# One more 2 MB load and store, in rows of 16 KB, ahead of everything else in a decode-attention backward kernel

## The chip, the core and the metric

The kernel runs on one core of a Trainium2 chip. Five engines work side by side: TensorE (PE, with its weight loads as PEld), VectorE (DVE), ScalarE (ACT), GpSimd (POOL) and SyncE (SP), which here issues nearly all transfers. Sixteen DMA engines move the data between HBM and the on-chip memory of 128 partitions. The metric is the device time of one execution in microseconds.

## What is computed

The reference is the forward pass and the gradients of a block that adds two branches to its input: attention of one new token over a cache, and a bilinear gated MLP.

```
def _A_ref(x, k_cache, v_cache, wq, wo):          # B=2, Sq=1, D=576, Hq=32, Hkv=16, Sk=4096, Dh=128
    q = (x @ wq).reshape(B, Sq, Hq, Dh).transpose(0, 2, 1, 3)
    k, v = jnp.repeat(k_cache, rep, axis=1), jnp.repeat(v_cache, rep, axis=1)      # rep = 2
    p = softmax(jnp.einsum("bhqd,bhkd->bhqk", q, k) * Dh ** -0.5)
    o = jnp.einsum("bhqk,bhkd->bhqd", p, v)
    return o.transpose(0, 2, 1, 3).reshape(B, Sq, Hq * Dh) @ wo
def _B_ref(x, w_gate, w_up, w_down):              # F = 4608
    return ((x @ w_gate) * (x @ w_up)) @ w_down
xn = layernorm(x)
out = x + _A_ref(xn, k_cache, v_cache, wq, wo) + _B_ref(xn, w_gate, w_up, w_down)
```

There are nine outputs: `out` (out_0) and the gradients by x (out_1), the key cache (out_2), the value cache (out_3), wq (out_4), wo (out_5), w_gate (out_6), w_up (out_7) and w_down (out_8). All is bfloat16. The two caches are 2 x 16 x 4096 x 128, 33.5 MB each, and so are their gradients; every gradient has the size of its input, so as many bytes are written as read.

## The kernel before, in words

**Steps.** The work on the caches is cut into 16 steps. A step is one group of two key heads (four query heads) of one of the two batch rows. For each step two heads of keys and two of values are loaded, 1 MB per head: partition p holds 32 consecutive positions, which is one row of 8 KB (`load_kv`, line 1078; the transfer is on line 1087). DVE transposes them in blocks (`turn`, through the helper on line 418), PE makes the scores (line 1205), the softmax runs on ACT and DVE, PE contracts the probabilities with the cache (line 1378), and PE makes the gradients of keys and values as outer products (line 1226). Their results stand in PSUM in pieces of 128 x 1024 and are copied to a big buffer by ACT or DVE (the helper `cp`, lines 422 and 424), whichever the planner picks, and stored from there (`put`, line 644). In between stand the groups of weights of attention (wq, wo) and nine slices of the MLP, whose gradients are outer products too.

**Buffers.** Sixteen big buffers of 8 KB per partition (`big`, line 368) are shared by four users: loaded keys and values (`kv`, at most 7 at a time), transposed copies (`X`, at most 15), results to be stored (`st`, at most 4) and gate or up weights (`G`, at most 2). A buffer is taken with ACQ and given back with REL, or, for a transfer, when the transfer has landed.

**Order.** All parts of the kernel are generators, which yield what they need next: an engine for an estimated time, a buffer, an event, a transfer. A planner (`Order`, line 64) runs them at build time against its own estimates and a table of priorities (`PRI`, line 256), takes what can start first, and so writes down the order of instructions on each engine. The order is fixed when the program is built; at run time each engine works through its list, and waits on semaphores. One added request can so move everything that is planned after it.

**Queues.** SP issues all transfers but two small ones of ACT, in one list. It does not pass over an entry: a store that waits for its eviction holds up the loads behind it. Transfers use eight completion semaphores in turn, so a transfer is issued only once the one eight places before it has landed. The list of before starts with the first head of keys, the first weights of wq and wo, the second head of keys and the first head of values, then two MB of gate and up weights and two slices of w_down, the second head of values, and the keys and values of the next step. The first store stands behind 20 transfers.

Of the kernel before, what the change touches and what calls it, by code (L numbers as in the profile page):

```python
# [12 lines left out]
BF16 = mybir.dt.bfloat16  # L13
P = 128
# [210 lines left out]
def ACQ(tag):  # L225
    return ("acq", tag)
# [6 lines left out]
def WAIT(*events):  # L233
    return ("wait", events)


def SET(event):
    return ("set", event)
# [6 lines left out]
def PRIO(prio):  # L245
    return ("prio", prio)


def DMA(engine, cost, nbytes, row=8192):
    return ("dma", engine, cost, 0.01 + RATE * nbytes / 16e3 * (0.03676 + 8.0 / row))  # L250
# [3 lines left out]
NBIG, NGU, NWW, NBD = 16, 1, 6, 3  # L254
# [51 lines left out]
def pr(name, i=0):  # L306
    return PRI[name][i]
# [3 lines left out]
def kernel(  # L311
# [22 lines left out]
    nc = tc.nc  # L334

    Bq, Sq, D = A_x.shape
    _, Hkv, Sk, Dh = A_k_cache.shape
# [8 lines left out]
    NCH = Sk // P  # L346
# [12 lines left out]
    const = ctx.enter_context(tc.tile_pool(name="const", bufs=1))  # L359
    ps = ctx.enter_context(tc.tile_pool(name="ps", bufs=1, space=bass.MemoryType.PSUM))  # L360

    od = Order()

    def tiles(tag, n, shape, dtype=BF16):
        od.ring(tag, n)
        return [const.tile(list(shape), dtype, name=f"{tag}{i}") for i in range(n)]

    kv_t = X_t = st_t = G_t = tiles("big", NBIG, [P, NCH * Dh])
    od.share("big", CAP)
    Xt_t = tiles("Xt", 1, [P, 2 * FS])  # L370
    gu_t = tiles("gu", NGU, [P, 4 * FS])
# [703 lines left out]
    views = [A.rearrange("b h (p c) d -> b h p (c d)", p=P) for A in (A_k_cache, A_v_cache)]  # L1075
    oviews = [A.rearrange("b h (p c) d -> b h p (c d)", p=P) for A in (out_2, out_3)]

    def load_kv():
        n = 0
        for s in range(NS):  # L1080
            g, b = divmod(s, Bq)
            for t in range(2):
                for l in range(G):
                    yield PRIO(pr("load", s) if n else -1e5)
                    i = yield ACQ("kv")
                    yield DMA("SP", 0.36, 1 << 20)
                    nc.sync.dma_start(kv_t[i][:], views[t][b, G * g + l])
                    kvS[s][t][l] = i
                    yield ("lset", kvL[s][t][l])
                    yield SET(issued[n])  # L1090
                    n += 1
# [48 lines left out]
    def load_ws(items):  # L1140
        for n, (gate, item) in enumerate(items):
            yield PRIO(pr("mload" if item[0] == "mlp" else "wload", n))
            yield ("gate", issued, gate)
            yield from load_w(item)

    def turn():
        for s in range(NS):
            for t in range(2):
                yield PRIO(pr(f"turn{t}", s))
                for l in range(G):  # L1150
                    yield WAIT(kvL[s][t][l], *([] if s + t == 0 else [grp[s // Bq]["Ed" if t else "Eq"]]))
                    x = yield ACQ("X")
                    src = kv_t[kvS[s][t][l]]
                    for h in range(2):
                        yield DVE(1.25)
                        t32(pairs(X_t[x][:, 2048 * h:2048 * h + 2048]), pairs(src[:, 2048 * h:2048 * h + 2048]))
                    xS[s][t][l] = x
                    yield SET(xE[s][t][l])

    def build_W(t):  # L1160
        for s in range(NS):
            g, b = divmod(s, Bq)
            yield PRIO(pr(f"W{t}", s))
            yield WAIT(Ezero)
            yield WAIT(grp[g]["Eq" if t == 0 else "Ed"])
            w = yield ACQ(f"W{t}")
            wS[s][t] = w
            for a in range(4):
                yield POOL(0.22)
                nc.gpsimd.tensor_copy(  # L1170
                    view(W_t[t][w][:], 32 * a, 32, 6 + 8 * a, [[G * WW, 4], [WW, G], [1, 2]]),
                    view(rep_t[grp[g]["qs"]][:], 32 * a, 32, t * 8 * GH + b, [[2 * GH, 4], [4, G], [2, 2]]))
            yield SET(wE[s][t])

    def build_BD():
        for s in range(NS):
            g, b = divmod(s, Bq)
            for t in (0, 1) if s == 0 else (1, 0):
                yield PRIO(pr(f"BD{t}", s))
                yield WAIT(Econst)  # L1180
                yield WAIT(*[grp[g][x] for x in (("Eq",) if s == 0 and t == 0 else ("Eq", "Ed"))])
                v = yield ACQ("vr")
                m = yield ACQ("m")
                yield PE(0.053)
                nc.tensor.matmul(m_t[m][:, 0:P],
                                 lhsT=qr_t[grp[g]["qs"]][:, t, b, :],
                                 rhs=ident[:], start=True, stop=True)
                e = yield EV(128)
                cp(e, vr_t[v][:], m_t[m][:, 0:P])
                yield REL("m", m)  # L1190
                i = yield ACQ("BD")
                yield POOL(3.6)
                nc.gpsimd.tensor_tensor(BD_t[i][:], view(vr_t[v][:], 0, P, 0, [[0, 16], [1, Dh]]),  # L1193
                                        view(mask16[:], 0, P, 0, [[1, 16], [0, Dh]]), ALU.mult)
                yield REL("vr", v)
                bS[s][t] = i
                yield SET(bE[s][t])
# [50 lines left out]
    def attend():  # L1248
        for s in range(NS):
            yield PRIO(pr("att", s))  # L1250
            yield WAIT(Econst)
            yield from softmax(s)
# [98 lines left out]
    def dscores():  # L1351
        for s in range(NS):
            yield PRIO(pr("dsc", s))
            yield from dscore(s)
# [50 lines left out]
    def backs():  # L1405
        for g in range(NG):
            yield PRIO(pr("back", g))
            yield WAIT(Emore, Exr)
            yield from group_back(g)

    def fronts():
        for g in range(NG):
            yield PRIO(pr("front", g))
            yield from group_front(g)
# [33 lines left out]
    def final_dx():  # L1448
# [46 lines left out]
    od.spawn(load_ws([it for g in range(NG) for it in (  # L1495
        (AT["wq"][g], ("wq", g)), (AT["wo"][g], ("wo", g)))]), -50.0, 0.2)
    od.spawn(load_ws([(AT["mlp"][i], ("mlp", i)) for i in range((NFS + 1) // 2)]), -50.0, 0.2)
    od.spawn(load_kv(), -1e5, 0.0)
    for gen in (turn(), fronts(), build_W(0), build_W(1), build_BD(), attend(), dscores(), backs()):
        od.spawn(gen, 0.0)  # L1500
# [33 lines left out]
```

## Time and profile before

| | before |
|---|---|
| median of two runs | 471.11 us (470.67 to 471.55) |
| profiled execution | 471.37 us |
| its span | 469.6 us |
| mean granted TensorE clock | 0.71 |
| bytes moved | 185.96 MB, mean 396 GB/s |
| data queue, share of 16 engines | 98.1% |
| busiest engines | PE 79%, DVE 79%, ACT 71%, POOL 31% |
| transfers of SP | 220 |

The span runs from the first to the last instruction of one profiled execution; its own time has some 1.8 us more around it. Busy shares are averages over the whole span. The DMA share is the mean over 16 engines of the time that packets were under way; since a packet's time holds its waiting and packets overlap a little, it can stand slightly above 1. In lists of waits, an entry names the engine and line that waited, the engine and line that ended the wait, the total, the number and the longest.

### The profile page before, as it was taken

Reading aid. Unit: us, or ns where it says so; the run is one execution under the profiler, and the core shown is the slowest. Engines: PE = TensorE matmul, PEld = TensorE weight load, DVE = VectorE, ACT = ScalarE, POOL = GpSimd, SP = SyncE. Lnnn points to the kernel's source line nnn. Section 1 sums busy time; section 2 is a strip of 40 time slices with the busy share of each in tenths; the row PEclk is TensorE's granted clock in tenths of the full one; section 3 lists DMA queues with packets and bytes.
Section 4 is the critical chain, followed back from the end, with each engine's and each line's share of the span. In section 5 each row is a group of like instructions: output and inputs, shape, how many; then the busy total and the mean of one; then the engine's idle time right before and its main releaser. Section 6 shows DMA issues by size and latency. Waiting matters only on the chain.

```text
span 469.6 us, 15459 instructions
## 1 busy us (share of the span) xinstructions
PE 370.8 (79%) x6636; PEld 217.5 (46%) x6636; DVE 369.5 (79%) x705; ACT 334.3 (71%) x507; POOL 146.8 (31%) x176
## 2 busy tenths in 40 slices
PE   0588688869887777986997669789699898998984
PEld 0455444435653352554463444564345434444453
DVE  9689878967867879688689658978867978898772
ACT  2149668867885948671798638877678678789973
POOL 3350242681330320203252264000843705325100
PEclk9978897767757668776675767956656658566977
DMA  8999999999999999999999999999999989999995
GB/s 317 404 413 403 363 390 419 409 416 421 418 416 420 399 421 406 412 415 419 399 418 404 386 418 424 408 413 342 413 416 393 424 270 416 423 413 413 424 368 176
DMA packets 40053, 185.96 MB, mean 396 GB/s; under 512 B 3496, under 2 KB 11184, under 8 KB 23600
## 3 DMA queue, kind: packets, MB, share of 16 engines
q1 hardware_dynamic: 39976, 184.96, 98.1%
q8 instruction: 52, 0.85, 0.7%
q14 instruction: 17, 0.14, 0.1%
q10 hardware_dynamic: 8, 0.00, 0.0%
HBM read 92.48 MB, written 92.48 MB: 394 GB/s over the span
## 4 chain that ended last, share of the span: by engine, by line
PE 42%; ACT 18%; DVE 18%; DMA 12%; issue 5%; POOL 2%; SPq 2%; ACTq 0%; DVEq 0%; POOLq 0%
ACT big L422 15%; DMA out_dram<-big 10%; DVE big L418 8%; PE ps_m L1378 8%; PE ps_o L1226 7%; PE ps_m L1205 7%; PE ps_o L675 4%; PE ps_m L841 3%; DVE big L424 3%; DMA big<-in_A_v_cache_dram 3%; PE ps_m L967 2%; PE ps_m L636 2%; POOL BD L1193 2%; PE ps_o L712 1%; SPq L1129 1%
## 5 line engine op out<-in xcount | busy, mean ns | idle before, releaser
L422 ACT CAST big<-ps_o 128x1024 bf16<-128x1024 f32 (+4 forms) x319 | 279.7, 950 | 40.3 <-PE ps_o L1226 18.2
L418 DVE STREAM_TRANSPOSE big<-big 128x1024 f32<-128x1024 f32 x146 | 176.1, 1223 | 5.9 <-DMA big<-in_A_v_cache_dram 3.6
L1193 POOL TENSOR_TENSOR BD<-vr,mask 128x2048 bf16<-128x2048 bf16 x32 | 115.2, 3603 | 198.8 <-ACT vr L422 122.2
L424 DVE CAST big<-ps_o 128x1024 bf16<-128x1024 f32 (+2 forms) x71 | 78.2, 1102 | 15.8 <-PE ps_o L675 5.2
L1205 PE MATMUL ps_m<-big,W 128*32 128x128 bf16 x2048 | 57.1, 274 | 5.5 <-ACT osb L422 0.7
L1226 PE MATMUL ps_o<-BD,dd 32*128 32x512 bf16 x256 | 48.8, 489 | 12.7 <-ACT big L422 9.2
L1205 PEld LDWEIGHTS <-W 128*32 128x32 bf16 x2048 | 45.4, 121 | 21.9 <-issue 18.6
L1226 PE MATMUL ps_o<-BD,pp 32*128 32x512 bf16 x256 | 42.1, 461 | 10.4 <-ACT big L422 6.7
L1170 POOL COPY W<-rep 32x16 bf16<-32x16 bf16 x128 | 24.5, 192 | 63.5 <-DVE rep L951 53.2
L418 DVE STREAM_TRANSPOSE big<-ww 128x1152 f32<-128x1152 f32 (+1 forms) x25 | 32.9, 1317 | 4.5 <-DMA out_dram<-big 3.3
L1378 PE MATMUL ps_m<-big,pp 128*32 128x512 bf16 x256 | 28.2, 536 | 1.5 <-DVE small L1330 1.2
L1378 PE MATMUL ps_m<-big,dd 128*32 128x512 bf16 x256 | 27.5, 518 | 1.5 <-DVE dd L418 0.6
L1226 PEld LDWEIGHTS <-dd 32*128 32x128 bf16 x256 | 11.8, 97 | 32.4 <-issue 24.7
L1226 PEld LDWEIGHTS <-pp 32*128 32x128 bf16 x256 | 10.4, 95 | 26.9 <-issue 22.6
L422 ACT CAST osb<-ps_m 128x512 bf16<-128x512 f32 x15 | 8.9, 590 | 15.9 <-PE ps_m L1378 12.6
L675 PE MATMUL ps_o<-dyr,R 32*32 32x288 bf16 x256 | 17.3, 402 | 2.0 <-ACT big L422 2.0
L675 PE MATMUL ps_o<-dyr,hb 32*32 32x288 bf16 x288 | 16.5, 346 | 1.1 <-ACT big L422 0.9
L967 PE MATMUL ps_m<-big,Wdy 128*128 128x128 bf16 x144 | 14.9, 285 | 3.1 <-DVE small L1283 2.0
L712 PEld LDWEIGHTS <-xnr 32*128 32x128 bf16 x368 | 12.5, 119 | 9.3 <-issue 8.6
L422 ACT CAST sp<-ps_m 128x256 bf16<-128x256 f32 x22 | 8.4, 380 | 11.2 <-PE ps_m L1213 11.0
L636 PEld LDWEIGHTS <-wm 128*32 128x32 bf16 x704 | 13.4, 115 | 6.3 <-issue 5.1
L841 PE MATMUL ps_m<-big,Wdy 128*128 128x128 bf16 x162 | 15.6, 272 | 0.6 <-DVE small L1291 0.4
(210 smaller groups left out, 481.9 us busy)
## 6 DMA issues: line engine op xcount, KB each, us to landing
out_dram<-big SPq DMA_DIRECT2D x74, 1024.0 KB, 12.1
big<-in_A_k_cache_dram SPq DMA_DIRECT2D x32, 1024.0 KB, 12.4
big<-in_A_v_cache_dram SPq DMA_DIRECT2D x32, 1024.0 KB, 12.5
out_dram<-big SPq DMA_DIRECT2D x17, 576.0 KB, 11.4
ww<-in_B_w_down_dram SPq DMA_DIRECT2D x9, 576.0 KB, 11.1
ww<-in_A_wo_dram SPq DMA_DIRECT2D x8, 576.0 KB, 11.1
ww<-in_A_wq_dram SPq DMA_DIRECT2D x8, 512.0 KB, 11.6
big<-in_B_w_gate_dram SPq DMA_DIRECT2D x4, 1024.0 KB, 13.1
```

Source lines behind the costliest of these rows:

```text
L418: nc.vector.transpose(out, in_)
L422: nc.scalar.copy(out, in_)
L424: nc.vector.tensor_copy(out=out, in_=in_)
L636: nc.tensor.matmul(dp[32 * q:32 * q + 32, :], lhsT=view(Wm[:], 0, P, 8 * pos(q, s), [[1, 32]]), rhs=view(X, 0, P, xoff(q, s), [[FS, blocks ...
L675: nc.tensor.matmul(o[32 * q:32 * q + 32, aa, 0:HD2], lhsT=view(t, 32 * q, 32, 2 * A + aa, [[4, 32]]), rhs=dyr[32 * q:32 * q + 32, k * HD2: ...
L841: nc.tensor.matmul(dh, lhsT=Wdy[:, e, 2 * k:2 * k + P], rhs=view(X[:], 0, P, 64 * k + e, [[D, FC], [2, 32]]), start=(k == 0 and e == 0), s ...
L967: nc.tensor.matmul(dp, lhsT=Wdy[:, e, 2 * k:2 * k + P], rhs=view(X[:], 0, P, 64 * k + e, [[D, GH], [2, 32]]), start=(k == 0 and e == 0), s ...
L1170: nc.gpsimd.tensor_copy(view(W_t[t][w][:], 32 * a, 32, 6 + 8 * a, [[G * WW, 4], [WW, G], [1, 2]]), view(rep_t[grp[g]["qs"]][:], 32 * a, 32 ...
L1193: nc.gpsimd.tensor_tensor(BD_t[i][:], view(vr_t[v][:], 0, P, 0, [[0, 16], [1, Dh]]), view(mask16[:], 0, P, 0, [[1, 16], [0, Dh]]), ALU.mult)
L1205: nc.tensor.matmul(sc[32 * cq:32 * cq + 32, :], lhsT=view(W[:], 0, P, (be * G + l) * WW + 6 - 4 * c2 - 2 * l, [[1, 32]]), rhs=view(X[:], 0 ...
L1226: nc.tensor.matmul(o[:, k, :], lhsT=pr2[32 * c4:32 * c4 + 32, :], rhs=BD[32 * c4:32 * c4 + 32, 8 * l + 4 * h2:8 * l + 4 * h2 + 4, :], star ...
L1378: nc.tensor.matmul(ct[32 * j:32 * j + 32, :], lhsT=view(rT, 0, P, 4 * c + 2 * l, [[1, 32]]), rhs=kv_t[kvS[s][t][l]][:, Dh * c:Dh * (c + 4) ...
```

## The change

A new generator `long_rows` is planned ahead of `load_kv`. It takes two neighbouring buffers, loads the first two heads of keys of batch row 0 into them with one transfer of 2 MB, waits until it has landed, and stores the same bytes with one transfer to the place of the last two heads of key gradients of batch row 1. These are written again later, by the stores of the last step, so what the kernel returns does not change. Each of the 128 rows of the two transfers is 16 KB long: partitions 0 to 63 take the first head and 64 to 127 the second, 64 positions each.

So that a row of 16 KB fits, the sixteen big buffers are now the halves of eight tiles of twice the size. Their number, their size and the caps of their users are the same. `load_kv` still loads the same heads of keys again for its own use.

```
-    kv_t = X_t = st_t = G_t = tiles("big", NBIG, [P, NCH * Dh])
+    pair_t = [const.tile([P, 2 * NCH * Dh], BF16, name=f"big{i}") for i in range(NBIG // 2)]
+    kv_t = X_t = st_t = G_t = [t[:, NCH * Dh * h:NCH * Dh * (h + 1)] for t in pair_t for h in range(2)]
+    od.ring("big", NBIG)
...
+    def long_rows():
+        yield PRIO(-2e5)
+        i = yield ACQ("kv")
+        j = yield ACQ("kv")
+        assert j == i + 1 and i % 2 == 0
+        two = pair_t[i // 2]
+        land = Event()
+        yield DMA("SP", 0.36, 2 << 20, 16384)
+        nc.sync.dma_start(two[:], A_k_cache[0, 0:2].rearrange("h (p c) d -> (h p) (c d)", p=P // 2))
+        yield ("lset", land)
+        yield WAIT(land)
+        yield DMA("SP", 0.36, 2 << 20, 16384)
+        nc.sync.dma_start(out_2[1, Hkv - 2:Hkv].rearrange("h (p c) d -> (h p) (c d)", p=P // 2), two[:])
+        yield ("lrel", "kv", i)
+        yield ("lrel", "kv", j)
...
+    od.spawn(long_rows(), -2e5, 0.0)
     od.spawn(load_kv(), -1e5, 0.0)
```

In the built order of the changed kernel the long load is SP's first transfer and the long store its ninth; between them stand the first two heads of keys, wq, wo, the first head of values and the first gate weights.

## The prediction

> **What bounds the kernel now.** I read the page from the outside in: first how full the DMA engines are, then where in the span they are not, and only then the engines and the chain. These are lines of the page of the kernel before: span, engine and slice rows, DMA queues, chain, two groups of evictions, and DMA issues with their time to landing.
>
> ```profile
> span 469.6 us, 15459 instructions
> PE 370.8 (79%) x6636; PEld 217.5 (46%) x6636; DVE 369.5 (79%) x705; ACT 334.3 (71%) x507; POOL 146.8 (31%) x176
> ...
> DMA  8999999999999999999999999999999989999995
> GB/s 317 404 413 403 363 390 419 409 416 421 418 416 420 399 421 406 412 415 419 399 418 404 386 418 424 408 413 342 413 416 393 424 270 416 423 413 413 424 368 176
> DMA packets 40053, 185.96 MB, mean 396 GB/s; under 512 B 3496, under 2 KB 11184, under 8 KB 23600
> ...
> q1 hardware_dynamic: 39976, 184.96, 98.1%
> q8 instruction: 52, 0.85, 0.7%
> ...
> HBM read 92.48 MB, written 92.48 MB: 394 GB/s over the span
> ...
> PE 42%; ACT 18%; DVE 18%; DMA 12%; issue 5%; POOL 2%; SPq 2%; ACTq 0%; DVEq 0%; POOLq 0%
> ...
> L422 ACT CAST big<-ps_o 128x1024 bf16<-128x1024 f32 (+4 forms) x319 | 279.7, 950 | 40.3 <-PE ps_o L1226 18.2
> ...
> L424 DVE CAST big<-ps_o 128x1024 bf16<-128x1024 f32 (+2 forms) x71 | 78.2, 1102 | 15.8 <-PE ps_o L675 5.2
> ...
> out_dram<-big SPq DMA_DIRECT2D x74, 1024.0 KB, 12.1
> ```
>
> The queue that carries the data was taken for 98.1% of the span, and no engine for more than 79%. The slice row says the same thing over time: a 9 everywhere but in the first slice, one in the middle and the last. The chain that ended last looks like compute (PE 42%, ACT 18%, DVE 18%), but I do not read it as the bound. Each load waits for a buffer that a reader frees, and each store for an eviction, so a chain followed back from the end runs through engines even while the DMA engines always have work.
>
> The windows (columns: stretch, length, busy time of PE, PEld, DVE, ACT, POOL, granted clock, DMA share, GB/s) show where the queue falls short.
>
> ```profile
> 0.00:1.90 1.90, 0.00 (x0) 0.00 (x0) 1.10 (x13) 0.32 (x1) 1.30 (x7) 1.00 0.17 31
> ...
> 0.00:35.26 35.26, 17.50 (x334) 12.35 (x334) 27.60 (x96) 11.29 (x25) 14.88 (x27) 0.90 0.96 378
> ...
> 5.00:455.00 450.00, 363.52 (x6450) 212.30 (x6453) 360.38 (x667) 326.45 (x495) 142.52 (x168) 0.71 1.01 405
> ...
> 200.00:300.00 100.00, 80.30 (x1442) 48.91 (x1442) 78.83 (x137) 69.55 (x111) 32.09 (x41) 0.69 1.01 410
> 300.00:400.00 100.00, 84.05 (x1372) 45.54 (x1369) 78.95 (x140) 74.98 (x110) 36.47 (x43) 0.64 0.98 387
> 400.00:455.00 55.00, 49.35 (x787) 25.97 (x783) 46.00 (x81) 47.23 (x68) 13.61 (x4) 0.69 1.02 418
> 455.00:469.60 14.60, 7.29 (x190) 5.13 (x190) 4.92 (x19) 6.40 (x10) 0.00 (x0) 0.73 0.52 182
> ...
> 375.00:380.00 5.00, 4.75 (x60) 2.19 (x58) 4.41 (x8) 3.50 (x5) 0.02 (x1) 0.50 0.59 204
> ```
>
> From 5 to 455 us the share is 1.01: packets lie back to back for 450 of 469.6 us, and in the middle I see one clear hole (375 to 380 us, share 0.59, so 0.41 x 5 = 2.1 us lost). Outside that stretch stand a start-up of about 2 us and a tail of 14.6 us at share 0.52. So bytes set this time: what is added to the queue is paid in full, unless it fills a hole.
>
> The profiled execution took 471.37 us by its own time, 1.8 us more than its span; the median of the runs is 471.11. They differ by 0.06%, so a sum on the profiled one stands for both. A measurement tells 2% from no change here: 9.4 us, or 480.5 us.
>
> **The change, part by part.** *Bytes.* Nothing is removed. Two DMAs come in: a load of 2 MB (2,097,152 bytes, 128 rows of 16 KB) and a store of the same size. The same keys are loaded a second time by the old loop, and the stored rows are overwritten by the last key gradients, so neither replaces other traffic. Together they are 4.19 MB, 2.3% of 185.96 MB.
>
> The price per byte of a 16 KB row of this queue stands in no row of the trace, so I bound it. From below, the best stretch: 400 to 455 us, mostly transfers of 1 MB in 8 KB rows, ran at 418 GB/s, which gives 4.19 / 0.418 = 10.0 us; slices reach 424 GB/s, 9.9 us. From above, the only packets of 16 KB in the trace: the instruction queue moved 52 of 0.85 MB, so 16 KB each, in 0.7% of 16 engines' span, or 0.007 x 16 x 469.6 / 52 = 1.01 us a packet; 256 of them on 16 engines are 16.2 us. The mean of the full stretch, 405 GB/s, gives 10.4. I take 10.0, from the data queue's own large rows: the instruction fetches are isolated packets that share each engine with this queue, so their time holds waiting.
>
> The Trainium skill, in "DMA: Bandwidth & Descriptors" under Specifications, gives about 358 GB/s of HBM per core and says that for HBM traffic this side binds; by it the term would be 11.7 us as an estimate and the sum 483.9 us. The trace disagrees, with 405 GB/s held over 450 us.
>
> *The two issues.* SP issues a transfer in about 0.34 us (the rows below); the median one lands 12.1 us after its issue, so the queue is several transfers deep and this costs nothing. If the queue were dry, it would cost 0.7 us.
>
> *The load stands first.* All other transfers start 2 MB later: 2.1 / 0.418 = 5.0 us. Nothing on the chip waits for these rows except their own store, but the first keys wait behind them. SP's own rows, and the first transpose of keys on DVE (start us, length, what):
>
> ```profile
> 8.31 1.23 DVE L418 STREAM_TRANSPOSE big<-big 128x1024 f32<-128x1024 f32 x1
> ...
> 35.26 0.34 SPq L644 DMA_DIRECT2D out_dram<-big  x1
> ...
> 39.07 0.34 SPq L644 DMA_DIRECT2D out_dram<-big  x1
> ```
>
> Compute so starts about 5 us later, which is part of the 10.0 us and not added to it: DMA is busy meanwhile. The danger is the first store that needs compute. SP issues in order, so a store that waits for an eviction holds back all loads behind it, and those feed DVE and PE. Before, 15.3 MB stand ahead of that store, which went out at 35.26 us, when 35.26 x 0.378 = 13.3 MB had moved: 2.0 MB in hand. In the built order of the changed kernel 16.3 MB stand ahead of it, and it is the value gradient that went out at 39.07 us before. The queue lasts until 35.26 + (16.3 - 13.3) / 0.405 = 42.7 us; the data come at 39.07 + 5.0 = 44.1 us at the latest, and earlier since the evictions of the MLP's store now come behind. The hole is 0 to 1.4 us; I take 0.8, about the middle.
>
> *The long store.* It stands ninth on SP, after three MB of keys, values and gate weights. Its load came first, so its wait is over when SP gets there; behind it are weight loads and the second half of the values. Until it lands, two of the seven buffers for keys and values and two of the sixteen big ones are missing. This moves no bytes, only their order, and loads fill the queue meanwhile. If the cover were gone, it would be one more wait of SP of the length below.
>
> *The order after that.* Instructions are laid out by a planner at build time, so all else may move. Counting bytes ahead of each transfer in both built orders: most of the 64 loads and 64 stores stand 4.2 MB further back, which is a plain shift; loads 45 to 50 stand 5.8 to 6.9 MB back, and loads 23 to 27 about where they were. Behind the last load of values 15.8 MB are left, before it was 16.8. About 12 evictions of the big buffers pass from ACT to DVE: 12 x 1.10 = 13 us more DVE work in 480 us, which is 80% in place of 79%. I cost this part at nothing, since DVE is not the bound; the price when it opens holes is the rival below. The tail (14.6 us at 0.52) I leave as it is.
>
> *Pair tiles.* A big buffer becomes half of a pair. In the built program no wait ties two halves of one pair to each other that are used separately, so they cost nothing.
>
> *Sum:* 471.4 + 10.0 (bytes) + 0.8 (first hole) = 482.2 us, 2.4% above.
>
> **The rivals.** *The bytes are partly absorbed.* The first keys come 5 us late and the whole queue is 10 us longer, so after the long store compute runs some 5 us ahead of the queue compared with before. SP's waits (us in total, times, longest) would shrink:
>
> ```profile
> SPq L644 <- ACT big L422: 112.3, 58, 6.9
> SPq L644 <- DVE big L424: 90.6, 36, 7.9
> SPq L1087 <- PE ps_m L1378: 16.5, 7, 7.8
> ```
>
> The wait of 7.8 us is the one that made the hole at 375 us. If that lead closed the holes, the stretch from 300 to 400 us would run at 410 GB/s like the one ahead of it, not at 387: 100 x (1 - 387/410) = 5.6 us back. The time would be 471.4 + 10.0 - 5.6 = 475.8 us, not slower by what can be told. It decides once more than 1.7 us come back. Against it: buffers, not engines, give the lead, and they are as many as before, so a lead is used up as soon as the buffers are full; and part of the low rate is small rows, not holes. By the same mechanism, with all of the shortfall against 418 GB/s returned (450 x (1 - 405/418) = 14.0 us), the time would be 467.4; 11,184 packets under 2 KB speak against that.
>
> *The new order opens holes.* A wait of SP longer than the queue is deep leaves the engines dry. The queue is 12.1 us deep at the median, the longest wait 7.9 us, and one of 7.8 us made the hole of 2.1 us. With loads 45 to 50 2 MB later and other stores ahead of loads, four such holes more are 8.4 us: 490.6 us. For it: 203 us of waits for evictions lie just under the surface, and each could surface. Against it: the shift by bytes is even.
>
> *Rows of 16 KB are slow.* At the price of the instruction packets: 471.4 + 16.2 + 0.8 = 488.4 us. Against it: those packets wait beside a full queue, and 8 KB at 418 GB/s are 8,192 x 16 / 418,000 = 0.31 us a packet, a third of 1.01 us for half the bytes.
>
> *It does less than it says.* If the two transfers cost only the delay of the first keys, the time would be 476.4 us; it needs idle DMA engines, of which the first slices show none after 1.9 us.
>
> **How the numbers follow.** Forecast 482.2 us: 0.60, its own range 480 to 485, of which about a tenth lies under 480.5. Absorbed: 0.15. New holes: 0.18. Slow rows: 0.05. Less than it says: 0.02. Slower by over 2% is 0.60 x 0.9 + 0.18 + 0.05 = 0.77; faster by over 2% (below 461.7) needs more back than any hole holds, 0.01; within 2% the rest, 0.22. For 8 in 10 the range reaches from 477.5, most of the absorbed case, to 489.5, most of the holes and the slow rows.
>
> **What would show it.** The queue's row: 189.1 MB in q1 and a share near 98%, with GB/s over 5 to 465 us near 405. The first transpose of keys near 13 us instead of 8.3. The long transfers: 256 packets of 16 KB, or 512 of 8 KB, and 5 us each in their stretch. Around 42 us a window with a share below 1. If windows in the middle show shares of 0.6 to 0.9 more often than before, the new order is at work; if 300 to 400 us rises above 400 GB/s, bytes are absorbed. I am wrong if the share stays at 98% and the time rises by clearly more or less than 10 us: then the rate of the rows, not the holes, has changed.

## The result and the profile after

The changed kernel took 493.31 us (median of two runs, 492.31 to 494.31), the kernel before 471.11 us. The ratio is 1.0471, with a 95% interval of 1.0371 to 1.0572: slower by 22.2 us, about twice the 11 us forecast and 3.8 us above the range. The profiled execution took 494.31 us, its span 492.5 us.

The page of the changed kernel: span, engines, slices, queue, and the two groups of evictions.

```profile
span 492.5 us, 15462 instructions
PE 376.3 (76%) x6636; PEld 214.3 (44%) x6636; DVE 384.5 (78%) x725; ACT 323.2 (66%) x487; POOL 147.3 (30%) x176
...
DMA  8997989999998999999989999999999979999995
GB/s 313 409 411 291 395 307 365 391 376 402 422 418 333 366 415 418 424 422 415 419 293 415 416 412 387 420 424 416 364 411 418 425 288 353 418 416 412 421 417 206
DMA packets 40341, 190.15 MB, mean 386 GB/s; under 512 B 3528, under 2 KB 11216, under 8 KB 23632
...
q1 hardware_dynamic: 40264, 189.16, 96.7%
...
L424 ACT CAST big<-ps_o 128x1024 bf16<-128x1024 f32 (+2 forms) x305 | 269.1, 957 | 63.5 <-PE ps_o L1244 39.0
...
L426 DVE CAST big<-ps_o 128x1024 bf16<-128x1024 f32 (+3 forms) x85 | 92.7, 1091 | 23.6 <-PE ps_o L677 7.4
```

The bytes came as announced: 189.16 MB in the data queue, and 40,264 - 39,976 = 288 packets more, of which 256 are the rows of 16 KB. But the queue is less full. Its share times the span gives 476.2 us of packet time, and 16.3 us without; before, 98.1% of 469.6 us were 460.7, and 8.9 without. So of the 22.9 us by which the span grew, 15.5 are packet time and 7.4 are time without packets. Two transfers of 2 MB, priced at 10.0 us of packet time, explain neither the rest of the 15.5 nor the 7.4. (Such sums carry some 2 us: another execution of the same lists, in the run with the nudged estimate below, has 98.1% of 471.4 us, or 462.4.) The slice row has several more digits below 9, spread over the run, and not only at the start.

The windows of the changed kernel (columns as before) show the worst places, and its list of SP's waits what SP stood at.

```profile
40.00:45.00 5.00, 4.11 (x37) 2.29 (x31) 4.21 (x7) 3.52 (x6) 2.73 (x1) 1.00 0.53 220
45.00:50.00 5.00, 5.00 (x138) 3.73 (x137) 2.97 (x6) 3.90 (x6) 0.88 (x1) 1.00 0.91 298
...
155.00:160.00 5.00, 3.57 (x65) 1.71 (x65) 4.91 (x7) 5.00 (x8) 2.19 (x1) 0.86 0.65 215
250.00:255.00 5.00, 2.66 (x22) 0.66 (x22) 5.00 (x6) 4.34 (x5) 0.00 (x0) 0.50 0.69 191
400.00:405.00 5.00, 4.17 (x104) 2.93 (x97) 4.82 (x10) 3.13 (x4) 2.61 (x1) 0.91 0.38 124
405.00:410.00 5.00, 4.02 (x47) 1.34 (x46) 3.90 (x11) 2.76 (x7) 0.77 (x4) 1.00 1.00 365
5.00:455.00 450.00, 347.07 (x6110) 196.51 (x6110) 357.62 (x655) 296.34 (x448) 139.96 (x168) 0.72 0.99 391
```

```profile
SPq L646 <- DVE big L426: 117.1, 42, 12.4
SPq L646 <- ACT big L424: 95.5, 61, 7.8
SPq L1105 <- PE ps_m L1396: 32.1, 9, 10.4
SPq L1105 <- DMA out_dram<-big: 31.9, 11, 12.4
```

From 5 to 455 us the rate is 391 GB/s, where it was 405. Before, SP's longest wait was 7.9 us. Now there are three of 10 to 12.4 us, and each stands beside a hole: the first, 12.4 us at a store that waits for DVE, ends in the hole at 40 us, and one of 10.4 us ends at the hole at 250 us. The hole at 155 us has no such wait. There SP sent four stores in the 15.2 us from 137.8 us on and then stood 4.2 us more, so several shorter waits in a row did the same. The long wait at 400 us is of another kind: SP's own rows around it (start us, length, what) show that nothing was issued for 12 us.

```profile
385.63 4.83 SPq L646 DMA_DIRECT2D out_dram<-big  x4
402.88 0.34 SPq L1105 DMA_DIRECT2D big<-in_A_v_cache_dram  x1
```

Here a load of values takes the buffer of a store that had just been issued, and so waits until that store has landed. Since SP issues nothing meanwhile, the queue drains almost to the end: share 0.38 from 400 to 405 us.

### The profile page after: what moved, and what is told of

The parts are those of the page before. It is cut to its first block, busy times and chain, and to the rows that moved or that the text cites. A ratio compares the mean times of both kernels' runs of the same rounds, so it can differ in the third digit from the quotient of the medians.

```text
span 492.5 us, 15462 instructions
## 1 busy us (share of the span) xinstructions
PE 376.3 (76%) x6636; PEld 214.3 (44%) x6636; DVE 384.5 (78%) x725; ACT 323.2 (66%) x487; POOL 147.3 (30%) x176
## 3 DMA queue, kind: packets, MB, share of 16 engines
q1 hardware_dynamic: 40264, 189.16, 96.7%
## 4 chain that ended last, share of the span: by engine, by line
PE 42%; ACT 18%; DVE 17%; DMA 15%; issue 7%; SPq 1%; DVEq 0%; ACTq 0%
ACT big L424 15%; DVE big L420 9%; PE ps_o L1244 8%; PE ps_m L1223 8%; PE ps_m L1396 7%; DMA big<-in_A_v_cache_dram 7%; PE ps_o L677 4%; DVE big L426 4%; DMA big<-in_A_k_cache_dram 3%; DMA ww<-in_A_wq_dram 3%; DMA out_dram<-big 3%; PE ps_m L969 2%; PE ps_m L638 2%; PE ps_m L843 1%; PE ps_o L714 1%
## 5 line engine op out<-in xcount | busy, mean ns | idle before, releaser
L424 ACT CAST big<-ps_o 128x1024 bf16<-128x1024 f32 (+2 forms) x305 | 269.1, 957 | 63.5 <-PE ps_o L1244 39.0
L426 DVE CAST big<-ps_o 128x1024 bf16<-128x1024 f32 (+3 forms) x85 | 92.7, 1091 | 23.6 <-PE ps_o L677 7.4
L1244 PE MATMUL ps_o<-BD,dd 32*128 32x512 bf16 x256 | 46.4, 464 | 11.8 <-ACT big L424 9.9
L1244 PE MATMUL ps_o<-BD,pp 32*128 32x512 bf16 x256 | 45.9, 502 | 10.6 <-ACT big L424 8.0
L1396 PE MATMUL ps_m<-big,pp 128*32 128x512 bf16 x256 | 29.2, 545 | 5.6 <-DMA big<-in_A_v_cache_dram 4.0
L985 POOL COPY qr<-qd 128x256 bf16<-128x256 bf16 x8 | 3.2, 397 | 54.1 <-DVE qd L426 53.5
L424 ACT CAST sp<-ps_m 128x256 bf16<-128x256 f32 x25 | 9.5, 381 | 13.2 <-PE ps_m L1231 11.0
L714 PEld LDWEIGHTS <-xnr 32*128 32x128 bf16 x368 | 12.7, 115 | 11.6 <-issue 10.9
L843 PEld LDWEIGHTS <-Wdy 128*128 128x128 bf16 x162 | 13.6, 121 | 5.9 <-issue 5.0
## 6 DMA issues: line engine op xcount, KB each, us to landing
out_dram<-big SPq DMA_DIRECT2D x74, 1024.0 KB, 12.7
big<-in_B_w_gate_dram SPq DMA_DIRECT2D x4, 1024.0 KB, 12.4
```

The source lines that it names most:

```text
L424: nc.scalar.copy(out, in_)
L426: nc.vector.tensor_copy(out=out, in_=in_)
L714: nc.tensor.matmul(o[:, aa, j * P:(j + 1) * P], lhsT=xnr[32 * a:32 * a + 32, dc * P:(dc + 1) * P], rhs=rhs(a), start=True, stop=True)
L843: nc.tensor.matmul(dh, lhsT=Wdy[:, e, 2 * k:2 * k + P], rhs=view(X[:], 0, P, 64 * k + e, [[D, FC], [2, 32]]), start=(k == 0 and e == 0), s ...
L1244: nc.tensor.matmul(o[:, k, :], lhsT=pr2[32 * c4:32 * c4 + 32, :], rhs=BD[32 * c4:32 * c4 + 32, 8 * l + 4 * h2:8 * l + 4 * h2 + 4, :], star ...
L1396: nc.tensor.matmul(ct[32 * j:32 * j + 32, :], lhsT=view(rT, 0, P, 4 * c + 2 * l, [[1, 32]]), rhs=kv_t[kvS[s][t][l]][:, Dh * c:Dh * (c + 4) ...
```

## The experiments

Three causes could give 22 us where 10 were priced. *New order*: the bytes cost their packets, the rest comes from the order that the planner laid out anew. *Rows*: the packets of 16 KB disturb the queue. *Late keys*: compute starts late and stays late. Medians and ratios are against runs of the kernel before on the same chip.

| run | median us | before us | ratio, 95% interval |
|---|---|---|---|
| old order, rows of 16 KB | 481.11 | 471.54 | 1.0218 (1.0183 to 1.0253) |
| old order, rows of 8 KB | 482.52 | 471.54 | 1.0235 (1.0210 to 1.0260) |
| new order, no bytes | 484.27 | 471.54 | 1.0268 (1.0216 to 1.0320) |
| latency estimate nudged | 471.72 | 471.54 | 1.0006 (0.9988 to 1.0025) |
| new order, one store later | 491.46 | 471.54 | 1.0416 (1.0390 to 1.0441) |
| no rows, rate estimate 0.3% up | 492.93 | 471.54 | 1.0452 (1.0413 to 1.0492) |
| no rows, drift estimate up | 482.17 | 471.54 | 1.0232 (1.0198 to 1.0265) |
| no rows, planned for late keys | 490.92 | 471.54 | 1.0433 (1.0392 to 1.0475) |
| old order, long load alone | 476.82 | 471.70 | 1.0109 (1.0075 to 1.0143) |
| old order, 13 evictions moved | 475.09 | 471.70 | 1.0068 (1.0037 to 1.0098) |
| new order, split as before | 496.05 | 471.70 | 1.0504 (1.0456 to 1.0551) |

### The bytes without the new order

The planner is not told of the long rows. Its order stays that of before on all engines, and the two transfers are put into SP's list at the places that they have in the changed kernel, through a pair of buffers that is still unused then.

```
+    def spd(dst, src):                     # stands in for every nc.sync.dma_start
+        spn[0] += 1
+        if spn[0] == 1:
+            nc.sync.dma_start(pair_t[7][:], A_k_cache[0, 0:2].rearrange("h (p c) d -> (h p) (c d)", p=P // 2))
+        if spn[0] == 8:
+            nc.sync.dma_start(out_2[1, Hkv - 2:Hkv].rearrange("h (p c) d -> (h p) (c d)", p=P // 2), pair_t[7][:])
+        nc.sync.dma_start(dst, src)
```

> The order of the kernel before on every engine, untouched; only the long load is put in as SP's first transfer and the long store as its ninth, in rows of 16 KB, through two buffers that nothing else uses before 29 us. Theory 'new order' (the bytes cost their packets, 10.7 us, and the other 12 us come from the order that the planner laid out anew): 480 to 484 us. Rival 'rows' (the long packets disturb the queue by more than their own time): 488 to 495 us. Rival 'late keys' (keys that come 5 us late make compute late for the whole run, whatever the order): 487 to 495 us.

The second run moves the same bytes with two loads and two stores of 1 MB, in rows of 8 KB.

> As the run with the old order and rows of 16 KB, but the same 2 MB are loaded and stored as two transfers of 1 MB each way, in rows of 8 KB. Theory 'new order': as with rows of 16 KB, 480 to 484 us. Rival 'rows': 480 to 483 us, 5 us or more below the run with rows of 16 KB. Rival 'late keys': 487 to 495 us, as with rows of 16 KB.

Measured: 481.11 and 482.52 us. Both rivals fall. Rows of 16 KB cost no more than rows of 8 KB (the intervals overlap), and keys that come late do not make the run late. The page of the run with rows of 16 KB, and its windows:

```profile
span 478.3 us, 15465 instructions
...
q1 hardware_dynamic: 40264, 189.16, 98.5%
```

```profile
40.00:45.00 5.00, 4.23 (x145) 2.47 (x137) 5.00 (x8) 4.56 (x8) 2.18 (x1) 0.99 1.00 408
45.00:50.00 5.00, 4.17 (x52) 2.15 (x47) 4.31 (x10) 3.99 (x6) 0.00 (x0) 0.70 1.05 402
```

The queue is as full as before: 471.1 us of packet time, 10.4 more than before, and 7.2 us without. The keys are just as late as in the changed kernel (the first transpose of keys starts at 11.23 us here and at 11.27 there), yet at 40 us there is no hole, since here the loads of the next step stand ahead of the first store.

### The new order without the bytes

```
-        nc.sync.dma_start(two[:], A_k_cache[0, 0:2].rearrange("h (p c) d -> (h p) (c d)", p=P // 2))
+        nc.sync.dma_start(two[:, 0:64], A_k_cache[0, 0:2].rearrange("h (p c) d -> (h p) (c d)", p=P // 2)[:, 0:64])
...
+        nc.sync.dma_start(out_2[1, Hkv - 2:Hkv].rearrange("h (p c) d -> (h p) (c d)", p=P // 2)[:, 0:64], two[:, 0:64])
```

> The changed kernel with its whole new order, but the long load and the long store move only the first 128 bytes of each row, 16 KB in all, so that they take next to no time and the stored copy is cut to that. Theory 'new order': 479 to 486 us, that is 8 to 15 us above the kernel before with the same bytes. Rival 'rows' and rival 'late keys': 470 to 474 us, since neither long packets nor late keys are left.

Measured: 484.27 us, 12.7 us above the kernel before with next to no bytes added.

```profile
span 481.5 us, 15460 instructions
...
q1 hardware_dynamic: 40264, 184.99, 96.8%
```

```profile
SPq L646 <- DVE big L426: 112.6, 40, 13.0
SPq L646 <- ACT big L424: 91.2, 56, 7.6
SPq L1105 <- DMA out_dram<-big: 26.3, 8, 13.1
SPq L1105 <- PE ps_m L1396: 22.2, 6, 10.5
```

The three long waits of the changed kernel are here again, with nearly the same lengths, though no key is late (the first transpose of keys starts at 8.30 us) and no long packet stands in the queue. Packet time is 466.1 us (5.4 more than before, or 3.7 more than in the other execution of the old lists), and 15.4 us are without packets (6.5 more). The two parts add up: 9.6 us for the bytes in the old order and 12.7 for the new order make 22.3, and the change cost 22.2. That they agree to 0.1 us is luck, since by the intervals each part is known to 2 or 3 us and the whole, from two runs, to 5.

The long load alone, in the old order, splits the first part once more.

> The old order with only the long load of 2 MB as SP's first transfer; the long store is left out. If bytes are paid in full, half of what load and store cost together in the old order (9.6 us): 475 to 477 us. If the late first keys are what costs, and the store hides: 479 to 482 us. If the load hides in the start and the store is what costs: 471 to 473 us.

Measured: 476.82 us, 5.1 us above, about half of 9.6. The late keys are inside these 5.1 us, not on top, and the store behind them costs its bytes too.

### Is it this order, or any new one?

Here the kernel has no long rows; only one estimate of the planner is changed.

```
-LATENCY, DRY, RATE = 0.5, 0.9, 1.009
+LATENCY, DRY, RATE = 0.52, 0.9, 1.009
```

> The kernel before without any long rows; only the planner's own estimate of a transfer's latency goes from 0.50 to 0.52 us, so that it lays out a somewhat different order for the same work. Theory 'new order', in the form that any order laid out anew opens holes: 476 to 486 us. In the form that only the order around the long rows does: 470 to 474 us. The rivals on rows and late keys: 470 to 474 us.

Measured: 471.72 us. This decides nothing, against what was expected of it: the built program has the same list on every engine. It serves as a second run of the kernel before, with a ratio of 1.0006. Three other estimates do give other lists:

```
-LATENCY, DRY, RATE = 0.5, 0.9, 1.009
+LATENCY, DRY, RATE = 0.5, 0.9, 1.012          # rate
...
-LM, LAG, DRIFT = 0.67, 2.2, 0.009
+LM, LAG, DRIFT = 0.67, 2.2, 0.0095            # drift
...
+    od.free["SP"] = 5.0                       # planned for late keys
```

> The kernel before without any long rows, but the planner's estimate of the rate goes from 1.009 to 1.012; this lays out a new order on every engine (the nudge of the latency had left every list as it was). Theory 'new order, any': 476 to 486 us, with holes in windows of the middle. Form 'only the order around the long rows': 470 to 474 us.

> The kernel before without long rows; the planner's estimate of how transfers fall behind goes from 0.0090 to 0.0095, which leaves SP's list alone up to the thirtieth load and lays out a new order behind it. Theory 'new order, any': 473 to 482 us, holes only in the second half. Form 'only the order around the long rows': 470 to 474 us.

> The kernel before without long rows; the planner is told that SP is busy for its first 5 us, so it lays out an order for keys that come 5 us late, which on the chip they do not. Theory 'new order, any': 475 to 485 us. Form 'only the order around the long rows': 470 to 475 us. Rival 'late keys': 470 to 475 us, since no key is late on the chip.

Measured: 492.93, 482.17 and 490.92 us. The first and the last are above what was expected even of "any new order", and the second stands at the upper end. With the order that only lost its bytes there are four orders laid out anew, and all four cost 10.6 to 21.4 us with next to no bytes more. The run with the rate changed, windows and SP's waits:

```profile
5.00:50.00 45.00, 29.79 (x606) 19.33 (x606) 36.88 (x99) 23.44 (x39) 10.62 (x19) 0.89 1.01 400
50.00:100.00 50.00, 37.86 (x656) 23.60 (x659) 40.46 (x75) 32.05 (x50) 19.36 (x28) 0.66 1.01 393
100.00:200.00 100.00, 81.56 (x1598) 51.12 (x1591) 79.12 (x139) 66.36 (x97) 30.61 (x35) 0.69 0.93 367
200.00:300.00 100.00, 82.14 (x1255) 44.07 (x1255) 78.82 (x140) 65.86 (x102) 30.64 (x41) 0.65 1.02 411
300.00:400.00 100.00, 81.90 (x1434) 46.88 (x1431) 83.54 (x145) 70.24 (x105) 31.41 (x33) 0.68 0.95 377
```

```profile
SPq L644 <- DVE big L424: 126.3, 49, 10.9
SPq L644 <- ACT big L422: 90.0, 54, 9.7
```

The start is untouched (400 GB/s from 5 to 50 us, 403 before), and the loss stands mostly from 100 to 200 and 300 to 400 us, with waits of SP longer than any before; behind 455 us some 11 us are without packets, where before there were 7. The run with the drift changed keeps SP's list of before for its first 96 transfers, up to 202 us. It is nearly as full as before up to there (the kernel before is the first line below) and loses behind it:

```profile
100.00:200.00 100.00, 80.10 (x1507) 48.90 (x1507) 76.65 (x133) 71.81 (x108) 23.83 (x27) 0.68 1.02 415
...
100.00:200.00 100.00, 79.74 (x1477) 48.42 (x1476) 74.64 (x131) 71.10 (x109) 26.01 (x29) 0.68 1.02 415
200.00:300.00 100.00, 76.13 (x1392) 45.91 (x1390) 82.52 (x144) 63.60 (x95) 31.90 (x41) 0.68 0.96 378
```

Its longest wait of SP is only 8.4 us, at loads that wait for a store to land; such waits come to 32.3 us in all, where they were 16.0 before. The old order with the long load alone has a wait of 8.5 us and pays only its bytes. So the length of the longest wait alone does not tell a good order from a bad one. From 376 to 395 us three shorter ones follow on each other, with 7.9, 5.8 and 4.5 us between transfers, and the shares are 0.57 and 0.64 from 385 to 390 and 390 to 395 us.

```profile
SPq L1087 <- DMA out_dram<-big: 32.3, 10, 8.4
```

### Can a single hole be closed?

In the changed kernel the first store of a value gradient is moved four places back in SP's list, behind the loads that stood behind it.

```
+        if spn[0] == 19:
+            held.append((dst, src))
+            return
         nc.sync.dma_start(dst, src)
+        if spn[0] == 23:
+            nc.sync.dma_start(*held.pop())
```

> The changed kernel with one entry of SP's list moved: the first store of a value gradient goes out four places later, behind the loads of values, wq, keys and wo that stood behind it; nothing else is moved. Theory 'new order', with the mechanism that a wait of SP longer than the queue is deep leaves the DMA engines dry: the share of 0.53 at 40 to 45 us rises above 0.9, SP's wait of 12.4 us for DVE goes, and 2 to 5 us come back, 488 to 491 us. Rival 'the hole is only a symptom' (compute is late, and the time is lost at the next store instead): 492 to 495 us.

Measured: 491.46 us, between the two ranges, and 1.9 us below the changed kernel by the medians, which the intervals do not separate. The windows of this run, and its queue:

```profile
40.00:45.00 5.00, 3.91 (x79) 2.84 (x83) 4.72 (x8) 3.75 (x6) 3.24 (x1) 1.00 0.99 405
45.00:50.00 5.00, 3.59 (x114) 2.48 (x103) 4.80 (x10) 4.60 (x7) 0.36 (x1) 0.93 1.06 411
...
55.00:60.00 5.00, 4.20 (x156) 2.46 (x154) 3.93 (x8) 4.35 (x5) 0.11 (x1) 0.89 0.79 297
60.00:65.00 5.00, 2.94 (x63) 1.81 (x62) 2.30 (x7) 2.35 (x5) 0.00 (x0) 0.79 0.90 310
```

```profile
span 490.5 us, 15463 instructions
...
q1 hardware_dynamic: 40264, 189.16, 96.8%
```

The hole at 40 us is closed, and no wait for DVE is longer than 8.2 us: the loads behind the waiting store were what the DMA engines lacked there. But over the run 15.7 us are without packets, where the changed kernel has 16.3: nearly all of what the hole gave is lost again, from 15 us later on. So this run shows what made the hole, and speaks as much for the rival that one hole is only a symptom.

### Is it the split of the evictions?

The orders laid out anew so far give DVE more evictions (85 in the changed kernel and 71 before), and most of SP's longest waits are for DVE. So the split was tested by itself, from both sides: 13 evictions moved to DVE in the old order (84 there), and a bias that gives the new order the old split.

```
+        if e == "ACT" and cols == 1024:
+            moved[0] += 1
+            if moved[0] % 18 == 0:
+                e = "DVE"
...
-BIAS = 0.21111771427708687
+BIAS = 0.4
```

> The old order and no long rows; 13 of the 319 evictions of ACT are put on DVE at their places in the old list, which gives the split between the two engines that the changed kernel has (306 and 84). Theory 'split' (the orders laid out anew are slow because DVE, which also transposes, has the more evictions, so that stores wait for it): 477 to 484 us. Rival 'sequence' (it is where each instruction and each transfer stands, not how many stand on which engine): 470 to 475 us.

> The changed kernel with a stronger bias of the planner against DVE, 0.40 in place of 0.21, so that the evictions are split as before, 319 on ACT and 71 on DVE; the order is laid out anew once more. Theory 'split': 480 to 485 us. Rival 'sequence': 485 to 497 us, like any other order laid out anew with the bytes on top.

Measured: 475.09 us and 496.05 us. Moved evictions cost 3.4 us in the old order, a little above the upper end for "sequence" and below that for "split". With the old split the changed kernel is not faster; its queue is no fuller, and a long wait for DVE is still there:

```profile
span 494.1 us, 15483 instructions
...
q1 hardware_dynamic: 40264, 189.16, 96.0%
```

```profile
SPq L646 <- DVE big L426: 90.8, 32, 12.7
```

The split may cost some microseconds, 3.4 as it was moved here, but by itself it does not account for the 12.7.

## Why the prediction was wrong, point by point

**What bounds the kernel: right.** The old order with the bytes put in is as full as before (98.5%) and 9.6 us longer.

**Bytes, 10.0 us: right.** 9.6 us by the medians of the run with the old order, 10.4 of packet time by its page. Those 10.4 us over 16 packets per engine are 0.65 us each, so the instruction packets of 1.01 us were indeed no price for long rows, and the rival of slow rows fell. So did the one by which the transfers cost only the delay of the first keys. The estimate of 11.7 us from the HBM limit, which the Trainium skill gives in "DMA: Bandwidth & Descriptors" under Specifications, is above both. That row works the limit out as half of 716 GB/s, for two cores; this kernel ran on one and held 391 GB/s over 450 us even with the change, so the limit did not bind here.

**The load stands first, 5.0 us: right in price, inside the sum.** 5.1 us for the load alone. The long store and the pair tiles, costed at nothing beyond their bytes, cost nothing more either: the old order has both in the run of 481.11 us. The first transpose of keys came less late than said. This is DVE's row of the changed kernel, with the idle time before it:

```profile
11.27 1.25 DVE L420 STREAM_TRANSPOSE big<-big 128x1024 f32<-128x1024 f32 x1 [2.88 <-DMA big<-in_A_k_cache_dram]
```

It is 3.0 us later than the 8.31 us of before, not 5: before, DVE was busy until then.

**The first hole, 0 to 1.4 us, taken 0.8: place right, size wrong.** The two windows lost 0.47 x 5 + 0.09 x 5 = 2.8 us. I had the queue last until 42.7 us and the data come at 44.1 us at the latest; SP's row of that store is

```profile
44.72 0.34 SPq L646 DMA_DIRECT2D out_dram<-big  x1
```

so the data came 0.6 us later than the latest time that I gave, and the loads behind it then still had to be issued and to reach the engines. This hole is no price of its own beside the next step: the run with the new order and no bytes has it too, with a share of 0.60 from 30 to 35 us behind its wait of 13.0 us.

**"The order after that", costed at nothing: the step that failed.** It cost 12.7 us. I read the shift of 4.2 MB in both lists as even, and as a sign that the plan was the same plan, shifted. It was not even: in the order in which SP issues them, only 27 of the 64 loads of keys and values stand 4.2 MB further back to within 0.3 MB, and the others from 2.4 MB ahead to 7.3 MB back. And the shift counts bytes ahead of a transfer; it says nothing of how long SP stands in front of each. In the order with the rate changed, which lost 21.4 us, most transfers stand within 2 MB of their old place. I also took the engines for a wide margin because they are 79% busy. The old order has only small margins: its waits of SP reach 7.9 us at a queue 12.1 us deep, and one of 7.8 already made a hole.

**The rival "the new order opens holes", 490.6 us at 0.18: what happened.** Its sign came too, windows in the middle with shares of 0.6 to 0.9. Its mechanism is shown for the longest waits: those of 10 to 13 us appear in the new order with and without the bytes, and stand beside holes. Holes also came behind shorter waits in a row, as at 155 us and in the run with the drift changed, which the rival did not have. Its price, four holes of 2.1 us, was too low: in the run without bytes 6.5 of the 12 us are time without packets, and some 4 to 5 are packets that took longer. Its chance was too low, too.

**The rival "absorbed": fell.** In the old order with the bytes the stretch from 300 to 400 us ran at 395 GB/s, not at 410, and the bytes were paid in full, 9.6 us of 10.0.

What stays open is which property of the old order makes it the good one. The table of priorities may have been set until this one order came out; that four of four other orders of the same work are slower agrees with it, but no run tests it. Nor does any run show that no order with the long rows is better than the old one with the bytes put in. No run was faster than the kernel before.

## What to carry to other kernels

Where a planner lays out the whole program, an added request has two prices: its own work, and the loss of the order that was there. Take them apart with two kernels, one that adds the work to the old order and one that takes the new order without the work. For a queue that issues in order, compare the waits of the issuer, the long ones and the short ones in a row, with the time that the queue holds, in the built order too: a store whose data are late, or a load into the buffer of a store just issued, empties the queue however even the bytes are spread.

## What the runs showed of the hardware that was not expected

After a hole the engines are fully occupied and yet slow. In the changed kernel the window from 405 to 410 us has a share of 1.00 and 365 GB/s, right behind the hole of share 0.38, where full stretches elsewhere in it reach 418 to 425. The kernel before has the same behind its one hole:

```profile
380.00:385.00 5.00, 5.00 (x65) 1.94 (x63) 2.74 (x7) 3.74 (x6) 0.00 (x0) 0.50 1.00 336
```

Over a run this may add up: the four other orders of the same work have 464.4 to 466.1 us of packet time, the two executions of the old lists 460.7 and 462.4. Two easy reasons fall. Rows are not smaller there: all packets of the window from 405 to 410 us are rows of 8 KB, with a median of 309 ns as in the whole run, but a mean of 356 where the whole run has 324, so some of them took much longer. And loads without stores are not slow by themselves: before, from 20 to 30 us, when no store had been issued yet, the rate was 420 GB/s. What makes some packets slow behind a hole stays open.
